# Late pieces of a spectral filter: scales by a product with ones, a fourth late piece, and earlier output units

## The chip, the cores and the metric

One core of a Trainium2 chip runs the whole program. The metric is the device time of one execution in microseconds; before the change the median of three runs is 583.74 us (583.57 to 584.98).

## The reference

Two independent halves, laid side by side in the last dimension of the output. Half A is attention with 16 query heads of 28 numbers and one shared key and value head over 2048 positions. Half B is a two-dimensional real Fourier transform of a 2048 x 448 array, a product with learned complex weights, and the transform back.

```python
# half A: S = 2048, D = 448, H = 16, Dh = 28
q = (x @ wq).reshape(B, S, H, Dh).transpose(0, 2, 1, 3)
k, v = x @ wk, x @ wv
p = softmax(einsum("bhqd,bkd->bhqk", q, k) * Dh ** -0.5)
a = einsum("bhqk,bkd->bhqd", p, v).transpose(0, 2, 1, 3).reshape(B, S, H * Dh) @ wo
# half B
X = rfft2(B_x) * (w_r + 1j * w_i)
b = irfft2(X, s=(S, D))
return concatenate([a, b], axis=-1)
```

## The kernel before

**First stage (to about 61 us).** TensorE multiplies x with the joined weights of queries, keys and values (L351). A small planner (`Plan`) orders these tasks with those of half B's first transform. Half B's input is cut into eight pieces `q` of 256 rows in the kernel's own order. A piece is folded on VectorE (`fold_part`), goes through the transform along the features on TensorE (`fa_task`, which calls `features`, L183, two halves `p`), is taken out by ScalarE, and goes through the first half of the transform along the positions (`fm_task`, which calls `fft1_mm`, L193). The result `bs` is stored to a DRAM array `t1`. `PLACES` names the products after which the pieces 0, 1 and 2 stand; piece 3 follows behind the last product, and of piece `L` = 4 only the features are done here. All of this is in float32.

**Main loop.** 256 steps: 16 groups (4 query blocks `c` by 4 head groups `g`) of 16 key blocks. A step is two score blocks (`scores`, L1317, 16 matmuls), two exps of 128 x 1024 on ScalarE (L1320) and a product with the values (`values`, L1336). Scores may run up to `PAIRS` = 9 blocks ahead. Each group gathers in one of two PSUM banks (`acc`), which alternate. When a group is done `group_out` (L1210) takes its bank out on VectorE, using a scale `scale_v`.

**Small units of work.** While a group gathers in one bank, the other may hold a filler unit: the late pieces of half B (`work["l"]`), output products (`work["w"]`, `w_unit`, L1255) and, towards the end, the transform back (`work["z"]`). `filler` says whether the bank is free, `owed` how much filler work is due by now, at the rates `EARLY` per step until the transform back has begun. All this is decided while the program is built: the loop keeps clocks for TensorE, VectorE and ScalarE, and `after(when, duration, function)` places VectorE's work at a time of that clock. Each engine then runs its list strictly in this order and waits where the real time differs.

**Late pieces.** For pieces 5, 6 and 7, in two float16 parts each: `late_top` finds each piece's largest value (L1009), `late_fold` folds (L165 to L173), `late_split` scales and splits (L1035, L1038), `late_features` multiplies (L1052, 48 matmuls), its `out` takes the bank out in two parts (L1061, L1062), `late_points` is the second transform (L1084; for piece `L` in float32) and its `out` scales and stores (L1092, L1094). The last piece starts `spectrum`: the rest of the transform, the product with the weights and the way back, all on VectorE.

**Maxima over partitions.** `bounce` writes a few columns of 128 maxima to DRAM (`md`), reads all of them back into each partition (`mw`) and reduces there (L922). It serves three times: for `late_top` (`mt`), for `largest` (`m`: values and output weights, from which `scale_v` comes) and for the spectrum (`mx`). The tile `mw` is single. SyncE issues these transfers, the query blocks (`qd` to DRAM and back into `qa`, `build_q`) and the stores of `bs`; GpSimd's queue issues the loads of weights and of the spectrum `X`.

**Output products.** Behind the last group of a block, `group_norm` sends leftover rows through DRAM (`lows`) and releases four `w_unit`s 7.0 us later by the clock.

Of the kernel before, what the change touches and what calls it, by code (L numbers as in the profile page):

```python
# [33 lines left out]
ROW = 32768.0  # L34
# [7 lines left out]
PLACES = (3, 5, 7)  # L42
# [59 lines left out]
def kernel(ctx: ExitStack, tc: tile.TileContext, t: dict):  # L102
# [32 lines left out]
    L = 4  # L135
    late, cs1 = {}, spare[1][1][:, :452].rearrange("p (j n) -> p j n", j=4)
    late["a", 4] = spare[1][0][:, 1024:1928]
    late["w", 4] = spare[0][1][:, 1416:1928]
    for q in range(5, 8):
        (one, two), o = spare[q > 5], 452 * (q > 5)  # L140
        if q < 7:
            late["x", q], late["W", q] = one[:, :1024], two[:, o:o + 512]
        late["f", q], late["A", q] = one[:, 1024:], two[:, o + 512:o + 1416]
# [99 lines left out]
    with tc.tile_pool(name="f1", bufs=2) as f1[0], tc.tile_pool(name="w1", bufs=1) as w1, ExitStack() as ctx1:  # L243
# [231 lines left out]
        for q in range(4):  # L475
            xb_load(q)

        def late_start():
            late_load(5, "xW")
            late_load(6, "xW")  # L480
            late_load(4, "w")
# [66 lines left out]
        for c in range(1, NC):  # L548
            for g in range(NG):
# [37 lines left out]
                if n in PLACES:  # L587
# [5 lines left out]
                    if q + 3 <= L:  # L593
                        xb_load(q + 3)
# [13 lines left out]
        fa_task(3, 0)  # L608
        fa_task(3, 1)
        ts = add(DVE, 0.2, lambda: terms(1, NC), kmb_, *(reds[a, b] for a in range(1, NC) for b in range(NG)))  # L610
        fm_task(2)
# [13 lines left out]
        fa_task(4, 0)  # L625
# [10 lines left out]
        fm_task(3)  # L636
# [3 lines left out]
        def last_features():  # L640
            pas[4, 1] = spin(2, 226)
            features(pas[4, 1], ff[4], 1)
# [84 lines left out]
        nc.vector.tensor_copy(late["a", 4][:, 1], pas[4, 1])  # L727
# [187 lines left out]
    def bounce(m, then, cols=2):  # L915
        d = dp.tile([128, cols], F32, name=f"md{cols}", bufs=2)
        nc.sync.dma_start(d, m[:, :cols])
        w = view(ap.tile([128, 384], F32, name="mw", bufs=1), 128, cols)
        nc.sync.dma_start(w, d.rearrange("(o a) b -> o a b", o=1).to_broadcast([128, 128, cols]))

        def go():
            V.tensor_reduce(m[:, :cols], w.rearrange("p a b -> p b a"), axis=AX.X, op=ALU.max)  # L922
            V.tensor_scalar(m[:, :cols], m[:, :cols], 1e-30, None, op0=ALU.max)
            then(m)
        after(clk["dve"] + 14.0, 1.0 if cols < 3 else 3.0, go)
# [76 lines left out]
    tops = {}  # L1002

    def late_top(qs):

        m = ap.tile([128, 8], F32, name="mt", bufs=1)
        V.memset(m, 0.0)
        for n, q in enumerate(qs):
            V.tensor_reduce(m[:113, n:n + 1], late["x", q][:113], axis=AX.XY, op=ALU.max, apply_absolute_value=True)  # L1009

        def fix(m):
            for n, q in enumerate(qs):
                tops[q] = ap.tile([128, 2], F32, name=f"t{q}", bufs=1)
                V.tensor_scalar(tops[q][:, 1:2], m[:, n:n + 1], 1.0 / ROW, None, op0=ALU.mult)
                V.reciprocal(m[:, 4:5], m[:, n:n + 1])
                V.tensor_scalar(tops[q][:, 0:1], m[:, 4:5], 4096.0, None, op0=ALU.mult)
# [4 lines left out]
    folded = set()  # L1021

    def late_fold(q, part=0):
        fold_part(late["x", q][:113], late["f", q][:113], part)
        if part < 2:
            after(clk["dve"], (1.22, 1.4)[part], late_fold, q, part + 1)
# [5 lines left out]
    def late_split(q, n):  # L1032
        f, x, scale = late["f", q][:113], late["F", q][:113], tops[q][:113, 0:1]
        if n == 0:
            V.tensor_scalar(x[:, 0], f, scale, None, op0=ALU.mult)  # L1035
            after(clk["dve"], 1.25, late_split, q, 1)
        else:
            STT(x[:, 1], f, scale, x[:, 0], op0=ALU.mult, op1=ALU.subtract)  # L1038
            work["l"].extend([late_features(q, 0), late_features(q, 1)])

    THREE = (0, 0), (0, 1), (1, 0)

    def late_features(q, p):
        def go(b):
# [10 lines left out]
            if q < 7 and p:  # L1055
                after(clk["pe"] + 1.8, 1.22, late_fold, q + 1)

        def out(b):
            a, pa = late["A", q][:, p], view(bank[b], 2, 226)
# [7 lines left out]
    def late_ready(q, p):  # L1067
        work["l"].insert(len(points), late_points(q, p))
        points.append((q, p))

    bsl, points = {}, []

    def late_points(q, p):
        def go(b):
            if q > L:
                points.remove((q, p))
# [9 lines left out]
            after(clk["pe"] + LAG, 0.6, out, b)  # L1086
        def out(b):
# [475 lines left out]
```

## Time and profile before

| | |
|---|---|
| profiled execution | 584.45 us; its span 582.7 us |
| TensorE (PE) busy | 571.4 us, 98% |
| ScalarE (ACT) busy | 512.7 us, 88% |
| VectorE (DVE) busy | 406.2 us, 70% |
| GpSimd (POOL) busy | 110.0 us, 19% |
| mean granted TensorE clock | 0.997 |
| HBM read, written | 44.64 MB, 19.98 MB |

A matmul in float32 leaves two records, one in float16 leaves one. Matmuls are pipelined, so durations of neighbours overlap; a distance from start to start tells more than a duration. A row of the timeline gives start, duration, engine, line, operation, tiles, and in brackets the idle time before it with what ended it. Rows that begin with two times and a colon give a stretch: its length, the busy time of PE, PEld, DVE, ACT and POOL with counts, then the granted TensorE clock, the DMA share and GB/s. The names of tiles that lie in shared memory (`spoh`, `spol`) are those of the buffer, not of the piece.

### The profile page before, as it was taken

What the parts mean: (1) busy time and instruction counts of PE and PEld (TensorE: products, weight loads), DVE (VectorE), ACT (ScalarE), POOL (GpSimd) and SP (SyncE); (2) the same over time, 40 slices, a digit from 0 to 9 for tenths busy, and PEclk for the clock granted to TensorE, in tenths of its full rate; (3) what the DMA queues carried; (4) which work ended last, traced back from release to release, by engine and by line L of the source; (5) the groups of instructions that cost most, each with busy time, mean ns of one, the idle gap of its engine ahead of it and who ended that gap; (6) DMA issues with size and microseconds to landing.
All of it is one profiled execution on the core that took longest, in us unless ns stands there. A gap on an engine that the chain in (4) does not pass through costs nothing.

```text
span 582.7 us, 20949 instructions
## 1 busy us (share of the span) xinstructions
PE 571.4 (98%) x9085; PEld 303.2 (52%) x9085; DVE 406.2 (70%) x775; ACT 512.7 (88%) x579; POOL 110.0 (19%) x199
## 2 busy tenths in 40 slices
PE   9999998999999999999999999999999999999996
PEld 7877543545454443444444444445555555555654
DVE  5996586789630999999898887845365743366544
ACT  4644897899999999999999999999999887899982
POOL 1023220121312012212111211133201321011110
PEclk9999999999999999999999999999999999999999
DMA  8864774244436202143302020456323342212111
GB/s 309 274 200 139 226 189 158 93 122 113 156 76 184 85 20 66 50 146 98 89 27 64 24 77 26 152 212 199 105 98 117 108 129 71 88 59 72 41 54 65
DMA packets 38935, 66.74 MB, mean 115 GB/s; under 512 B 7188, under 2 KB 29084, under 8 KB 38832
## 3 DMA queue, kind: packets, MB, share of 16 engines
q1 hardware_dynamic: 30008, 39.38, 20.9%
q0 software_dynamic: 8688, 25.76, 15.1%
q8 instruction: 72, 1.18, 0.9%
q14 instruction: 23, 0.19, 0.1%
q10 hardware_dynamic: 144, 0.23, 0.1%
HBM read 44.64 MB, written 19.98 MB: 111 GB/s over the span
## 4 chain that ended last, share of the span: by engine, by line
PE 77%; DMA 5%; DVE 4%; issue 1%; ACT 1%; SPq 0%; POOL 0%; DVEq 0%; ACTq 0%; POOLq 0%
PE banks L1317 34%; PE banks L1336 33%; PE banks L1255 6%; DMA mw<-md 2%; PE banks L1153 2%; PE banks L1179 2%; DMA qd<-qh 1%; DVE peaks L899 1%; DMA sd<-qraw 1%; DMA wo<-wo 0%; PE banks L1052 0%; DVE spoh L1038 0%; PE banks L1084 0%; DMA md<-mt 0%; ACT yb L1267 0%
## 5 line engine op out<-in xcount | busy, mean ns | idle before, releaser
L1320 ACT ACTIVATE p<-banks 128x1024 f32<-128x1024 f32 x512 | 477.0, 1101 | 29.7 <-PE banks L1317 29.2
L1317 PE MATMUL banks<-qa,ka 128*32 128x512 f16 x4096 | 277.1, 380 | 0.6 <-PEq L651 0.4
L1336 PE MATMUL banks<-p,vs 128*32 128x512 f32 x2048 | 268.9, 594 | 0.0
L1317 PEld LDWEIGHTS <-ka 128*32 128x32 f16 x4096 | 129.6, 96 | 168.8 <-issue 125.3
L1336 PEld LDWEIGHTS banks<-p,vs 128*32 128x32 f32 x2048 | 70.1, 110 | 43.0 <-issue 2.0
L1255 PE MATMUL banks<-woh,o 128*32 128x448 f16 x464 | 39.7, 353 | 1.2 <-DMA o<-lows 1.2
L1215 POOL DMA_DIRECT2D sd<-qraw x15 | 9.8, 651 | 154.1 <-DVE qraw L1210 154.0
L1255 PEld LDWEIGHTS <-o 128*32 128x32 f16 x720 | 23.8, 97 | 26.0 <-issue 19.6
L1223 POOL DMA_DIRECT2D R<-rd x60 | 30.5, 516 | 35.7 <-DMA rd<-rs 35.6
L865 DVE SCALAR_TENSOR_TENSOR X<-w,X 128x226 f32<-128x226 f32 (+2 forms) x72 | 34.0, 473 | 2.4
L1260 DVE TENSOR_SCALAR ya<-banks,scales 128x448 f32<-128x448 f32 x12 | 8.2, 684 | 25.5 <-PE banks L1255 25.4
L1186 DVE TENSOR_SCALAR w<-banks,scales 128x256 f32<-128x256 f32 x16 | 7.7, 484 | 25.9 <-PE banks L1179 25.8
L1210 DVE TENSOR_SCALAR qraw<-banks,scales 128x512 f32<-128x512 f32 x15 | 11.2, 749 | 20.4 <-PE banks L1336 20.4
L1255 PE MATMUL banks<-wol,o 128*32 128x448 f16 x256 | 24.8, 352 | 0.0
L1221 POOL DMA_DIRECT2D rd<-rs x15 | 8.2, 549 | 84.4 <-DVE rs L1220 72.7
L351 PE MATMUL banks<-xh,wqh 128*128 128x512 f32 x64 | 24.0, 406 | 0.0
L355 ACT ACTIVATE qraw<-banks 128x512 f32<-128x512 f32 x16 | 9.3, 596 | 16.0 <-PE banks L351 15.9
L351 PE MATMUL banks<-xh,wql 128*128 128x512 f32 x64 | 23.0, 389 | 0.0
L823 DVE TENSOR_TENSOR X<-X 128x904 f32<-128x904 f32 (+2 forms) x10 | 9.1, 906 | 18.2 <-DMA X<-t 18.2
L858 DVE SCALAR_TENSOR_TENSOR w<-X 128x113 f32<-128x113 f32 (+2 forms) x56 | 17.6, 354 | 0.1
L351 PE MATMUL banks<-xl,wqh 128*128 128x512 f32 x48 | 17.3, 390 | 0.0
L939 DVE TENSOR_TENSOR w<-X,wf 128x904 f32<-128x904 f32 x16 | 17.0, 1097 | 0.2
(182 smaller groups left out, 556.5 us busy)
## 6 DMA issues: line engine op xcount, KB each, us to landing
qa<-qd SPq DMA_DIRECT2D x62, 128.0 KB
ob<-yo SPq DMA_DIRECT2D x16, 256.0 KB
t<-bs SPq DMA_DIRECT2D x16, 226.0 KB
w<-w POOLq DMA_DIRECT2D x8, 452.0 KB, 6.0
X<-t POOLq DMA_DIRECT2D x8, 452.0 KB, 8.0
wf<-w POOLq DMA_DIRECT2D x8, 452.0 KB, 3.9
x<-t POOLq DMA_DIRECT2D x8, 452.0 KB, 4.5
R<-rd POOLq DMA_DIRECT2D x60, 56.0 KB, 2.2
```

Of the source, the lines that this page charges most:

```text
L351: mm(pq[c, g], w[:, j, gs], x[:, j], start=(j == 0 and n == 0), stop=(j == 3 and n == 1))
L858: STT(out, y, sy, x, op0=ALU.mult, op1=ALU.add if c > 0 else ALU.subtract)
L865: todo(226 * n, lambda d=d, q=q: STT(both(d), t[0].rearrange("p r n f -> p r (n f)"), q, both(a), op0=ALU.mult, op1=ALU.add))
L939: TT(u[r], both(s), wt[k][:, r:r + 1].to_broadcast([128, 2, 452]), op=ALU.mult)
L1153: mm(pz[r, j], fb["c2", q % 2][:, x, e, j, r], fb["fi", q % 2][:, j, f], start=(n == 0), stop=(n == 2))
L1179: mm(py[m:m + 32, k].rearrange("p (j n) -> p j n", j=4), cs3[:w, kind, f, m:m + 32], fb["z", q % 2, e][:w, x, :, 64 * r:64 * r + 64], star ...
L1210: V.tensor_scalar(o, bank[b], scale_v, None, op0=ALU.mult)
L1223: nc.gpsimd.dma_start(R[32 * i:32 * i + DH], rd[i:i + 1].to_broadcast([DH, CW]))
L1255: mm(p[r:r + 32], x[c][:, g, s][:, r:r + 32], w[:, m], start=(g == 0 and n == 0), stop=(g == NG - 1 and n == 2))
L1317: mm(bank[b + h][r], ka[:, k:k + 32], qa[c, g][:, 2 * p + h], start=True, stop=True)
L1320: nc.scalar.activation(pt[i], banks[:, b:b + 2], AF.Exp, scale=SCALE / UP / UP)
L1336: mm(bank[b][32 * i:32 * i + 32], vs[:, kc], pt[2 * st + i // 2][:, i % 2], start=(kc == 0), stop=(kc == 15))
```

## The change

- `L` becomes 3 and `PLACES` 4 and 7: pieces 0 and 1 stand behind products 4 and 7, piece 2 behind the last one, and piece 3 takes the place that piece 4 had. Pieces 5, 6, 4, 7 (`SEQ`) are late; they share two sets of buffers in turn, and the inputs of 4 and 7 are loaded at the start of the main loop.
- `late_top` works on two pieces at a time. The maxima `m` of 113 partitions are multiplied with a tile of ones (four matmuls of two columns, a new unit of the main loop, put at the head of `work["l"]`), which gives each partition their sum, and the scales come from the sum instead of the maximum. `bounce` is left with its two other users.
- Each late piece's fold is queued behind the split of the piece before it instead of behind its features.
- The first load of the filter weights is queued later (20.0 instead of 14.0), output units are released 8.0 instead of 7.0 behind the last normalization, and a unit may begin two steps into a group even when nothing is owed.

```diff
-PLACES = (3, 5, 7)
+PLACES = 4, 7
-    L = 4
+    L = 3
+    SEQ = 5, 6, 4, 7
...
     def late_top(qs):
-        m = ap.tile([128, 8], F32, name="mt", bufs=1)
-        V.memset(m, 0.0)
-        for n, q in enumerate(qs):
-            V.tensor_reduce(m[:113, n:n + 1], late["x", q][:113], axis=AX.XY, op=ALU.max, apply_absolute_value=True)
-        def fix(m):
-            for n, q in enumerate(qs):
-                tops[q] = ap.tile([128, 2], F32, name=f"t{q}", bufs=1)
-                V.tensor_scalar(tops[q][:, 1:2], m[:, n:n + 1], 1.0 / ROW, None, op0=ALU.mult)
...
-        bounce(m, fix, 3)
+        m = ap.tile([128, 4], F32, name="mt")
+        n = len(qs)
+        for i, q in enumerate(qs):
+            V.tensor_reduce(m[:113, i:i + 1], late["x", q][:113], axis=AX.XY, op=ALU.max, apply_absolute_value=True)
+        def go(b):
+            for r in range(0, 128, 32):
+                mm(bank[b][r:r + 32, :n], ones[:113, r:r + 32], m[:113, :n], start=True, stop=True)
+            after(clk["pe"] + LAG, 0.6, out, b)
+        def out(b):
+            t = ap.tile([128, 2, 2], F32, name="tops")
+            V.tensor_scalar(t[:, 0, :n], bank[b][:, :n], 1e-30, 2.0 ** -12, op0=ALU.max, op1=ALU.mult)
+            free[b] = clk["dve"] + 0.1
+            V.tensor_scalar(t[:, 1, :n], t[:, 0, :n], 4096.0 / ROW, None, op0=ALU.mult)
+            V.reciprocal(t[:, 0, :n], t[:, 0, :n])
...
+        after(clk["dve"] + 0.2, 0.0, work["l"].appendleft, (0.1, go))
...
-                after(clk["dve"] + 7.0, 0.0, work["w"].extend, [w_unit(c, k) for k in range(4)])
+                after(clk["dve"] + 8.0, 0.0, work["w"].extend, [w_unit(c, k) for k in range(4)])
...
-    after(14.0, 0.0, weight_top, 0)
+    after(20.0, 0.0, weight_top, 0)
-    for n, size in (("x", 1024), ("W", 512)):
-        shaped(n, 7, ap.tile([128, size], F32, name=n + "7", bufs=1))
-        late_load(7, n)
-    after(6.0, 3.4, late_top, (5, 6, 7))
-    after(6.1, 1.22, late_fold, 5)
+    ones = ap.tile([128, 128], F32, name="one", bufs=1)
+    after(2.0, 0.2, V.memset, ones, 1.0)
+    for q in SEQ[2:]:
+        for n, size in (("x", 1024), ("W", 512)):
+            shaped(n, q, ap.tile([128, size], F32, name=f"{n}{q}", bufs=1))
+            late_load(q, n)
+    after(6.0, 2.4, late_top, SEQ[:2])
+    after(6.1, 1.22, late_fold, SEQ[0])
+    after(28.0, 2.4, late_top, SEQ[2:])
...
+        if st % 16 == 2 and work["w"] and not fb:
+            owed = max(owed, 0.01)
```

By the order of the built programs the filler units of the first groups stand so (number of value steps ahead of the unit). Before: the two point units of piece 4 at 0 and 4, then features at 18 and 19, and further late units up to 51; the first output unit at 84. After: a point unit of piece 3 at 0, the first product with ones at 4, a point unit at 6, features at 8, points at 11, features at 13, the second product with ones at 19, and further late units up to 54; the first output unit at 85.

SyncE at the start of the main loop, before, from the load of the feature matrix on (`x_976`, `W_978` are the inputs of piece 7):

```order
L212 DMA spol<-cs 128x904
L212 DMA x_976<-xb 128x1024
L212 DMA W_978<-fz 128x1024
L226 DMA qd<-qh 128x512
L226 DMA qd<-ql 128x512
L229 DMA qa_79<-qd 32x4x512 x4
L917 DMA md_1092<-mt 128x3
L919 DMA mw<-md_1092 128x384
L917 DMA md_1158<-m 128x2
L919 DMA mw<-md_1158 128x256
L206 DMA t_83<-bs 256x1x226 x2
```

The same place after (`x_911`, `W_913` belong to piece 4, `x_915`, `W_917` to piece 7):

```order
L213 DMA spol<-cs 128x904
L213 DMA x_911<-xb 128x1024
L213 DMA W_913<-fz 128x1024
L213 DMA x_915<-xb 128x1024
L213 DMA W_917<-fz 128x1024
L227 DMA qd<-qh 128x512
L227 DMA qd<-ql 128x512
L230 DMA qa_79<-qd 32x4x512 x4
L916 DMA md<-m 128x2
L918 DMA mw<-md 128x256
L207 DMA t_83<-bs 256x1x226 x2
```

The trip of `mt` is gone, two loads came in ahead of `qd`, and the store of `bs` behind `mw` is now that of piece 3, from which GpSimd's first four loads of `X` read.

VectorE around the scales from `largest` and the emptying of group 0's bank, before (L922 to L800 make the scales, L1035 and L1038 are the two splits of piece 5, L1210 empties the bank):

```order
L1035 TENSOR_SCALAR spoh<-spoh,t_1357 113x1024
L922 TENSOR_REDUCE m<-mw 128x2
L923 TENSOR_SCALAR m<-m 128x2
L793 TENSOR_SCALAR m<-m 128x1
L794 TENSOR_SCALAR m<-m 128x2
L795 TENSOR_TENSOR scales<-m 128x1
L796 RECIPROCAL m<-m 128x2
L797 COPY scales<-m 128x1
L798 TENSOR_SCALAR scales<-scales 128x1
L799 TENSOR_TENSOR scales<-scales,m 128x1
L800 TENSOR_TENSOR scales<-scales 128x1
L1038 SCALAR_TENSOR_TENSOR spoh<-spoh,t_1357 113x1024
```

What stands ahead of those scales after (L1042 is the second split of piece 5, L1067 and L1068 take its first features out, L1100 its first points, L921 begins the scales):

```order
L1042 SCALAR_TENSOR_TENSOR spoh<-spoh,tops 113x1024
L1067 TENSOR_SCALAR spol<-banks 128x452
L1068 SCALAR_TENSOR_TENSOR spol<-banks,spol 128x452
L166 TENSOR_TENSOR spoh<-spoh 113x16x32 x2
L168 TENSOR_TENSOR spoh<-spoh 113x512
L169 TENSOR_TENSOR spoh<-spoh 113x512
L1100 TENSOR_SCALAR bs<-banks,tops 128x4x113
L171 TENSOR_TENSOR spoh<-spoh 113x256
L172 TENSOR_TENSOR spoh<-spoh 113x256
L173 TENSOR_TENSOR spoh<-spoh 113x256
L174 TENSOR_TENSOR spoh<-spoh 113x256
L921 TENSOR_REDUCE m<-mw 128x2
```

And what stands between those scales and the emptying of the bank after (L1008 finds the maxima of pieces 4 and 7, L898 that of a block of weights, L1039 and L1042 split piece 6, L1219 empties the bank):

```order
L1008 TENSOR_REDUCE mt<-x_911 113x1
L1008 TENSOR_REDUCE mt<-x_915 113x1
L898 TENSOR_REDUCE peaks<-w 128x1
L1039 TENSOR_SCALAR spoh<-spoh,tops 113x1024
L773 TENSOR_SCALAR woh<-wo,scales 128x448
L775 SCALAR_TENSOR_TENSOR wol<-wo,scales,woh 128x448
L1067 TENSOR_SCALAR spol<-banks 128x452
L1068 SCALAR_TENSOR_TENSOR spol<-banks,spol 128x452
L219 TENSOR_SCALAR qt<-qraw,mask,cvec 128x512
L220 CAST qh<-qt 128x512
L221 TENSOR_TENSOR ql<-qt,qh 128x512
L1042 SCALAR_TENSOR_TENSOR spoh<-spoh,tops 113x1024
```

L1219 is the next row. The whole first late piece moved ahead of the scales, and two reductions, a peak, a first split and an eviction moved in between the scales and the emptying of the bank.

More of the change, by code (lines that the diff above doesn't have):

```diff
@@ L133, in spin @@
         return view(bank[next(turn) % 6], *dims)
-    L = 4
+    L = 3
+    SEQ = 5, 6, 4, 7
     late, cs1 = {}, spare[1][1][:, :452].rearrange("p (j n) -> p j n", j=4)
[L137 to L141, printed above, removed]
+    late["a", L] = spare[1][0][:, 1024:1928]
+    late["w", L] = spare[0][1][:, 1416:1928]
+    for i, q in enumerate(SEQ):
+        (one, two), o = spare[i % 2], 452 * (i % 2)
+        if i < 2:
             late["x", q], late["W", q] = one[:, :1024], two[:, o:o + 512]
@@ L474 @@
         ident_ = load_const("ident", [128, 128])
-        for q in range(4):
+        for q in range(L + 1):
             xb_load(q)
         def late_start():
-            late_load(5, "xW")
-            late_load(6, "xW")
-            late_load(4, "w")
+            for q in SEQ[:2]:
+                late_load(q, "xW")
+            late_load(L, "w")
         late_ = add(SP, 2.4, late_start, xbl[3], kb=1800, due=45.0)
@@ L635 @@
                          cm, ident_)
[L636 removed]
+        fm_task(2)
         add(PE, 1.2, turn_values_all, users[-6], ident_, *krow_, *fetched["v"], bt_)
@@ L1025, in late_fold @@
         if part < 2:
-            after(clk["dve"], (1.22, 1.4)[part], late_fold, q, part + 1)
+            after(clk["dve"] + 0.8, (1.22, 1.4)[part], late_fold, q, part + 1)
         else:
@@ L1039, in late_split @@
             work["l"].extend([late_features(q, 0), late_features(q, 1)])
+            if q != SEQ[-1]:
+                after(clk["dve"] + 2.0, 1.22, late_fold, SEQ[SEQ.index(q) + 1])
     THREE = (0, 0), (0, 1), (1, 0)
@@ L1054, in go @@
             after(clk["pe"] + LAG, 1.3, out, b)
-            if q < 7 and p:
-                after(clk["pe"] + 1.8, 1.22, late_fold, q + 1)
         def out(b):
+            i = SEQ.index(q)
+            assert i < 2 or (SEQ[i - 2], p) in gone
             a, pa = late["A", q][:, p], view(bank[b], 2, 226)
@@ L1067, in late_ready @@
     def late_ready(q, p):
-        work["l"].insert(len(points), late_points(q, p))
-        points.append((q, p))
-    bsl, points = {}, []
+        work["l"].insert(len(ready), late_points(q, p))
+        ready.append((q, p))
+    bsl, gone = {}, set()
     def late_points(q, p):
         def go(b):
+            gone.add((q, p))
             if q > L:
-                points.remove((q, p))
+                ready.remove((q, p))
             pb = view(bank[b], 2, 226)
```

60 lines of the change are left out of this document (29 added, 31 removed).

## The prediction

> **What bounds the kernel now.** I read the busy times first, then the waits of the bottleneck engine, then the rows at the one place where it stands still. TensorE (PE) is almost never idle and ScalarE (ACT) comes next:
>
> ```profile
> PE 571.4 (98%) x9085; PEld 303.2 (52%) x9085; DVE 406.2 (70%) x775; ACT 512.7 (88%) x579; POOL 110.0 (19%) x199
> ```
>
> So the time is PE's work plus the few microseconds in which PE is slow or stands. A step of the main loop (16 score matmuls, 8 records of the value matmul) takes PE 1.72 us when nothing holds it (116.28 to 118.00 below). Where there is no other work, exp on ACT holds it: 79.70 to 96.18 is nine steps in 16.48 us, 1.83 each. The place to see is right behind that:
>
> ```profile
> 61.70 1.05 PE L1317 MATMUL banks<-qa,ka 128*32 128x512 f16 x16 [0.42 <-PEq L651]
> ...
> 64.96 1.04 PE L1336 MATMUL banks<-p,vs 128*32 128x512 f32 x8
> ...
> 71.19 0.95 PE L1084 MATMUL banks<-spoh,spol 128*32 128x226 f32 x16
> ...
> 79.70 0.61 PE L1336 MATMUL banks<-p,vs 128*32 128x512 f32 x4
> ...
> 96.18 1.04 PE L1336 MATMUL banks<-p,vs 128*32 128x512 f32 x8
> 100.12 0.80 PE L1052 MATMUL banks<-spol,spoh 113*32 113x113 f16 x48 [2.90 <-DVE qraw L1210]
> 100.73 2.22 PE L1317 MATMUL banks<-qa,ka 128*32 128x512 f16 x24
> 102.70 1.96 PE L1336 MATMUL banks<-p,vs 128*32 128x512 f32 x8
> 104.40 0.97 PE L1052 MATMUL banks<-spol,spoh 113*32 113x113 f16 x48
> 105.18 1.49 PE L1317 MATMUL banks<-qa,ka 128*32 128x512 f16 x24
> 106.47 1.05 PE L1336 MATMUL banks<-p,vs 128*32 128x512 f32 x8
> ...
> 116.28 1.05 PE L1336 MATMUL banks<-p,vs 128*32 128x512 f32 x8
> ...
> 118.00 1.04 PE L1336 MATMUL banks<-p,vs 128*32 128x512 f32 x8
> ```
>
> PE wants to put a late piece's features (L1052) into the accumulator bank of group 0 and must wait until VectorE (DVE) has emptied it (L1210). Behind the wait the clock is halved:
>
> ```profile
> 102.00:104.00 2.00, 2.00 (x20) 0.69 (x15) 1.32 (x3) 2.00 (x3) 0.00 (x0) 0.50 0.43 130
> ```
>
> (the third number from the right, the granted clock: 0.50). From 96.18 to 106.47 PE does two value steps (1.72), six score blocks of 8 matmuls (a quarter of a step each, 2.58) and two feature units (0.61 each): 5.52 us of work in 10.29, so 4.77 us are lost. Why DVE was late, from DVE, the chain of work and the SyncE queue (SPq):
>
> ```profile
> 66.81 2.35 DVE L1009 TENSOR_REDUCE mt<-spoh 113x1 f32<-113x1024 f32 x2
> 73.09 1.22 DVE L1009 TENSOR_REDUCE mt<-x 113x1 f32<-113x1024 f32 x1 [3.94 <-DMA x<-xb]
> 75.95 2.07 DVE L788 TENSOR_REDUCE m<-w 128x1 f32<-128x896 f32 x2
> 88.00 0.74 DVE L1035 TENSOR_SCALAR spoh<-spoh,t 113x1024 f16<-113x1024 f32 x1
> 93.43 0.42 DVE L922 TENSOR_REDUCE m<-mw 128x2 f32<-128x256 f32 x1 [4.69 <-DMA mw<-md]
> 95.39 1.28 DVE L1038 SCALAR_TENSOR_TENSOR spoh<-spoh,t 113x1024 f16<-113x1024 f32 x1
> 99.33 0.74 DVE L1210 TENSOR_SCALAR qraw<-banks,scales 128x512 f32<-128x512 f32 x1
> 101.07 1.09 DVE L899 TENSOR_REDUCE peaks<-w 128x1 f32<-128x904 f32 x1
> 102.72 0.63 DVE L1062 SCALAR_TENSOR_TENSOR spol<-banks,spol 128x452 f16<-128x452 f32 x1
> ```
>
> ```profile
> 65.98 8.08 DMA qd<-qh
> ...
> 76.30 2.23 DMA md<-mt
> ...
> 88.68 4.66 DMA mw<-md
> ```
>
> ```profile
> 78.93 0.42 SPq L917 DMA_DIRECT2D md<-m  x1
> ```
>
> Two trips through DRAM go through one queue and one buffer: first the late pieces' maxima (mt), then the maxima of values and output weights (m). The second write is issued at 78.93 and its read only at 88.68, 9.7 us later, and DVE, strictly in order, stands 4.69 us for it.
>
> **The change part by part.** Offsets from the first score matmul are written T0 (61.70 before).
>
> *One piece less in the first stage.* PE runs there without a gap:
>
> ```profile
> 40.25 1.76 PE L183 MATMUL banks<-spol,f 113*32 113x113 f32 x64
> 41.95 0.99 PE L193 MATMUL banks<-a,fw 64*64 64x226 f32 x16
> 42.87 0.50 PE L351 MATMUL banks<-xh,wqh 128*128 128x512 f32 x1
> ```
>
> From the start of the features (40.25) to the next L351 (42.87) one piece costs 2.62, and one such set of rows goes. All the rest of that stage hangs on PE. Term: -2.62.
>
> *The same piece in the main loop*, as two feature units and two point units (PE, starts to starts):
>
> ```profile
> 165.43 0.80 PE L1052 MATMUL banks<-spol,x 113*32 113x113 f16 x48
> 166.04 1.48 PE L1317 MATMUL banks<-qa,ka 128*32 128x512 f16 x24
> ...
> 168.19 0.77 PE L1084 MATMUL banks<-spol,W 128*32 128x226 f16 x24
> 168.77 0.59 PE L1317 MATMUL banks<-qa,ka 128*32 128x512 f16 x5
> ```
>
> 2 x 0.61 + 2 x 0.58 = +2.38. The two products with ones are new, four matmuls of two columns each. Nearest row, one product with four columns:
>
> ```profile
> 52.30 0.28 PE L521 MATMUL banks<-prod,blk 128*128 128x4 f32 x2
> ```
>
> Side by side in their four column groups 0.28, one after another 1.1; I take 0.4, near the first, since other units of four such blocks overlap. Twice: +0.8 (0.6 to 2.2).
>
> *Slack taken up.* Before, nothing but scores and values ran between 79.70 and 96.18, and ACT held PE for 9 x 0.11 = 0.98. Now five small units stand between steps 4 and 19: a product with ones (0.4), the float32 point unit that stood at step 3 (L1084 at 71.19, about 0.8 of its 0.95), two feature units and a point unit, 3.0 us in all, more than the slack. Term: -0.98. The piece's cost is thus partly hidden; where late units end (step 54) ACT binds PE as it did before from step 51, and I change nothing there.
>
> *No trip for mt.* DVE loses the 3.94 wait for the seventh piece and the third reduction, so m is ready about 5 us earlier, at T0 + 11.3 (before, L788 ended at 78.0 = T0 + 16.3). But its write does not leave earlier, because of what stands ahead of it on SyncE. In the rows of SyncE shown with the change the pair for mt is gone and 768 KB (x and W of one more piece) came in ahead of qd. The queues moved 269 GB/s while these loads ran:
>
> ```profile
> 62.00:72.00 10.00, 9.84 (x156) 4.64 (x152) 5.39 (x9) 9.59 (x11) 1.65 (x3) 1.00 0.89 269
> ```
>
> so qd lands 2.9 us later, at T0 + 12.4 + 2.9, the four qa issues take 2.2 (74.06 to 76.30), and md leaves at T0 + 17.5 (before T0 + 17.2). [...] From there md takes between 2.23 (first trip) and 9.7 (second). GpSimd's queue had four X loads of 452 KB in flight beside the second; these now include the piece that is stored behind mw in SyncE's rows, so they start later. I take 3, and mw 4.7: data at T0 + 25.2.
>
> When does DVE ask for it? By its rows shown with the change, the first late piece is split (L1042), evicted (L1067) and half through its points (L1100) ahead of L921; before, its two splits stood around the corresponding L922. L1100 needs the point unit that PE runs after 11 value steps: T0 + 3.3 (64.96) + 11 x 1.72 + 2.4 of small units = T0 + 24.6; with about 2 us of eviction and fold L921 is due near T0 + 26.7, with 1.5 to spare. From it to the end of the emptying of the bank (L1219, before L1210) the list has: the scales (93.43 to 95.39, 1.96), two reductions (2.35), one peak, one first split, one eviction (about 3.0 by L899, L1035 and twice L1062) and the work of 95.39 to 100.07 (4.68): 12.0, T0 + 38.7. PE needs the bank first for the second product with ones, after 19 steps: T0 + 3.3 + 32.7 + 3.0 = T0 + 39.0. So the 4.77 goes. Behind it DVE's list is full for some 30 steps and each unit waits for the eviction of the last, so I put +1.0 (0 to 2) for it, in which I also count this later stall (and drop it as a term, -0.72):
>
> ```profile
> 123.41 0.70 PE L1052 MATMUL banks<-spol,spoh 113*32 113x113 f16 x40 [0.72 <-DVE spoh L1038]
> 227.39 0.37 PE L1255 MATMUL banks<-woh,o 128*32 128x448 f16 x4 [1.19 <-DMA o<-lows]
> ```
>
> *Output units.* The first waited 1.19 for rows through DRAM (second row); they are now released 1 us later: -0.9 (0 to -1.2). Beginning them at step 2 of a group costs and gains nothing: the same 2.09 us in every 16 steps. The filter's spectrum comes some five steps later, so the final units crowd towards the end; PE is full there either way: 0 (-0.3 to +1).
>
> Sum: -2.62 + 2.38 + 0.8 - 0.98 - 4.77 - 0.72 + 1.0 - 0.9 = **-5.8 us**. The profiled execution took 584.45 (span 582.7, the rest lies around it and stays), 0.71 above the median of the runs, and would take 578.6; against the median of 583.74 I forecast **577.9**.
>
> **The rivals.** (a) The remaining trip still comes late and the stall stays about as it was: if md takes 7 to 8 us, PE stands some 3 us and the clock falls again. Then -5.8 - 1.0 + 4.8 = -2.0: 581.7. For it: 9.7 in the trace, and 768 KB more. Against it: the X loads are held back. The halved clock followed a wait of only 2.90. The Trainium skill, "TensorE: Matmul & The Clock Gate", section "Why this matters for your kernels", asks for no idle gap above about 3 us; the trace agrees with 2.90 and 0.50, and by either a 1 us wait stays at full clock.
> (b) Slower: md takes the full 9.7 or more, and mw lands near T0 + 33, over 6 us behind its place. DVE carries everything behind L921, so PE stands 7 us and runs 2 to 3 us more at half clock: -6.8 + 9.5 = +2.7, 586.4. It turns slower where wait and cold clock exceed 6.8, about 4 us behind its place. For it: DVE's in-order list; against: no DMA of that size took so long without the X loads.
> (c) The first stage does not shorten, because a load or the branch ends it: +2.6, 580.5. Against: PE has no wait there but 0.42 at the branch.
>
> **How the numbers follow.** Forecast 0.64, (a) 0.20, (c) 0.06, (b) 0.07, a gain eaten by small waits to within 0.3% (1.75 us, about what a measurement can tell from no change) 0.03. (a) and (c) are mostly faster than 582.0: faster 0.85, same 0.08, slower 0.07. The forecast's own terms give 575.7 to 579.7; to hold 8 in 10 the range goes up into (a): 575.4 to 581.6.
>
> **What would show it.** Right: first score near 59.0; no PE wait above 1.5 us behind a bank's emptying; clock 1.00 between 90 and 110; L921 without a wait; the first output unit without one. Wrong: a wait of L921 above 2 us with 0.50 behind it (a or b), or a first score later than 60.

## The result and the profile after

The changed kernel takes 580.07 us (median of 12 runs, 578.89 to 582.33) against 583.9 us for the kernel before beside it: ratio 0.9925, 95% interval 0.9903 to 0.9947, about 4.4 us faster. The forecast was 577.9 with a range of 575.4 to 581.6; the sign and the range hold, and the median lies 2.2 us above the forecast. The profiled execution took 579.96 us, its span is 578.2. The medians below leave out three executions in a slower state: one each of e3_both and e12_pad82 (745 us, granted clock near 0.75) and one of e5_before_banks (589.63 us). Line numbers moved: scores L1326, values L1345, late features L1058, late points L1091, the emptying of a group's bank L1219, output units L1264.

PE's busy row and its timeline where the forecast wanted the first score near 59.0:

```profile
PE 568.2 (98%) x9165; PEld 297.0 (51%) x9165; DVE 412.0 (71%) x779; ACT 510.1 (88%) x575; POOL 108.9 (19%) x199
```

```profile
57.46 0.99 PE L184 MATMUL banks<-spol,f 113*32 113x113 f32 x32
60.61 2.68 PE L1326 MATMUL banks<-qa,ka 128*32 128x512 f16 x24 [2.17 <-DVE spoh L726]
63.06 1.48 PE L1091 MATMUL banks<-spoh,spol 128*32 128x226 f32 x16
...
65.23 1.03 PE L1345 MATMUL banks<-p,vs 128*32 128x512 f32 x8
```

The last features end at 58.45 instead of 61.27, 2.82 us earlier. But PE then stands 2.17 us until VectorE's copy L726, and it runs at half clock behind that (0.50 in the window from 62 to 64 below, third number from the right). The first value step is at 65.23, before at 64.96: the first stage gave nothing. The copies that PE waits for, on VectorE, and the first of them before the change:

```profile
57.96 0.69 DVE L722 COPY vs<-banks 128x512 f32<-128x512 f32 x1 [2.15 <-DVEq L650]
58.68 1.22 DVE L507 TENSOR_TENSOR ka<-kf,ka 32x1024 f16<-32x1024 f32 x1
59.93 0.63 DVE L726 COPY spoh<-banks 128x452 f32<-128x452 f32 x1
```

```profile
60.25 0.69 DVE L723 COPY vs<-banks 128x512 f32<-128x512 f32 x1 [1.75 <-PE banks L617]
```

The name behind the 2.15 (`DVEq`, VectorE's sequencer) points at the branch, which both kernels pass here. Most of that wait is older than the change, though: the same copy waited 1.75 before, for the turned values that PE makes ahead of the last features.

At the old stall, and at the next one, PE and the windows:

```profile
94.12 1.04 PE L1345 MATMUL banks<-p,vs 128*32 128x512 f32 x8
94.98 1.05 PE L1326 MATMUL banks<-qa,ka 128*32 128x512 f16 x16
96.30 1.06 PE L1345 MATMUL banks<-p,vs 128*32 128x512 f32 x8 [0.28 <-DVE spol L1068]
98.05 1.04 PE L1345 MATMUL banks<-p,vs 128*32 128x512 f32 x8
...
100.63 0.22 PE L1012 MATMUL banks<-mt,one 113*32 113x2 f32 x8
100.69 1.04 PE L1326 MATMUL banks<-qa,ka 128*32 128x512 f16 x16
...
109.02 1.04 PE L1345 MATMUL banks<-p,vs 128*32 128x512 f32 x8
112.53 0.80 PE L1058 MATMUL banks<-spol,spoh 113*32 113x113 f16 x48 [2.47 <-DVE bs L1100]
113.14 1.49 PE L1326 MATMUL banks<-qa,ka 128*32 128x512 f16 x24
114.44 1.05 PE L1345 MATMUL banks<-p,vs 128*32 128x512 f32 x8
```

```profile
62.00:64.00 2.00, 2.00 (x26) 0.94 (x20) 0.00 (x0) 2.00 (x3) 0.43 (x1) 0.50 0.89 213
94.00:98.00 4.00, 3.73 (x56) 1.46 (x52) 3.86 (x8) 4.00 (x6) 0.00 (x0) 1.00 0.03 11
112.00:114.00 2.00, 1.47 (x64) 1.10 (x67) 2.00 (x6) 0.13 (x1) 0.00 (x0) 1.00 0.13 29
```

The stall of 4.77 us is gone, the clock is 1.00 there, and a product with ones delays the next scores by 0.06 us (100.63 to 100.69). Instead PE loses 2.65 us between 109.02 and 114.44 (5.42 for 2.77 of work). Why, from VectorE, GpSimd and SyncE:

```profile
87.98 0.44 DVE L921 TENSOR_REDUCE m<-mw 128x2 f32<-128x256 f32 x1
99.00 0.75 DVE L1219 TENSOR_SCALAR qraw<-banks,scales 128x512 f32<-128x512 f32 x1
107.56 0.45 DVE L773 TENSOR_SCALAR woh<-wo,scales 128x448 f16<-128x448 f32 x1 [4.06 <-DMA wo<-wo]
111.80 0.68 DVE L1100 TENSOR_SCALAR bs<-banks,tops 128x452 f32<-128x452 f32 x1
```

```profile
87.38 2.12 POOL L807 DMA_DIRECT2D X<-t  x4 [12.98 <-DMA t<-bs]
100.04 0.60 POOL L1224 DMA_DIRECT2D sd<-qraw  x1 [10.54 <-DVE qraw L1219]
104.15 0.56 POOL L1225 DMA_DIRECT2D rs<-sd  x1 [3.51 <-DMA sd<-qraw]
104.70 1.06 POOL L770 DMA_DIRECT2D wo<-wo  x2
```

```profile
74.20 0.38 SPq L916 DMA_DIRECT2D md<-m  x1
81.68 0.34 SPq L918 DMA_DIRECT2D mw<-md  x1
```

VectorE waits 4.06 us for a load of output weights that GpSimd issues only at 104.70, behind a store (`sd`) that waited for VectorE and a load (`rs`) that waited for that store. From there VectorE has no gap up to L1100, the eviction for which PE waits. The remaining trip's write took 7.5 us (74.20 to 81.68, until its read was issued), and yet L921 has no wait.

### The profile page after: what moved, and what is told of

It is laid out like the page before. It is cut to its first block, busy times and chain, and to the rows that moved or that the text cites. A ratio compares the mean times of both kernels' runs of the same rounds, so it can differ in the third digit from the quotient of the medians.

```text
span 578.2 us, 21096 instructions
## 1 busy us (share of the span) xinstructions
PE 568.2 (98%) x9165; PEld 297.0 (51%) x9165; DVE 412.0 (71%) x779; ACT 510.1 (88%) x575; POOL 108.9 (19%) x199
## 4 chain that ended last, share of the span: by engine, by line
PE 83%; DVE 3%; DMA 1%; ACT 1%; issue 1%; POOL 0%; ACTq 0%; DVEq 0%; POOLq 0%
PE banks L1326 37%; PE banks L1345 36%; PE banks L1264 6%; PE banks L1162 2%; PE banks L1188 2%; PE banks L1091 1%; PE banks L1058 1%; DMA sd<-qraw 1%; DVE peaks L898 1%; ACT p L1329 1%; DMA wo<-wo 0%; DVE mt L1008 0%; ACT yb L1276 0%; DVE ka L507 0%; DVE spoh L1042 0%
## 5 line engine op out<-in xcount | busy, mean ns | idle before, releaser
L1326 PE MATMUL banks<-qa,ka 128*32 128x512 f16 x4096 | 275.0, 380 | 2.2 <-DVE spoh L726 2.2
L1345 PE MATMUL banks<-p,vs 128*32 128x512 f32 x2048 | 267.4, 592 | 0.3 <-DVE spol L1068 0.3
L1326 PEld LDWEIGHTS <-ka 128*32 128x32 f16 x4096 | 126.5, 97 | 168.6 <-issue 119.9
L1345 PEld LDWEIGHTS banks<-p,vs 128*32 128x32 f32 x2048 | 68.0, 110 | 44.4 <-issue 1.2
L1264 PE MATMUL banks<-woh,o 128*32 128x448 f16 x464 | 39.8, 352 | 0.0
L1264 PEld LDWEIGHTS <-o 128*32 128x32 f16 x720 | 22.2, 97 | 27.1 <-issue 19.3
L1219 DVE TENSOR_SCALAR qraw<-banks,scales 128x512 f32<-128x512 f32 x15 | 11.2, 749 | 22.1 <-PE banks L1345 22.1
L1264 PE MATMUL banks<-wol,o 128*32 128x448 f16 x256 | 24.2, 352 | 0.0
L857 DVE SCALAR_TENSOR_TENSOR w<-X 128x113 f32<-128x113 f32 (+2 forms) x56 | 17.5, 355 | 0.1
```

Source lines behind the costliest of these rows:

```text
L857: STT(out, y, sy, x, op0=ALU.mult, op1=ALU.add if c > 0 else ALU.subtract)
L1219: V.tensor_scalar(o, bank[b], scale_v, None, op0=ALU.mult)
L1264: mm(p[r:r + 32], x[c][:, g, s][:, r:r + 32], w[:, m], start=(g == 0 and n == 0), stop=(g == NG - 1 and n == 2))
L1326: mm(bank[b + h][r], ka[:, k:k + 32], qa[c, g][:, 2 * p + h], start=True, stop=True)
L1345: mm(bank[b][32 * i:32 * i + 32], vs[:, kc], pt[2 * st + i // 2][:, i % 2], start=(kc == 0), stop=(kc == 15))
```

## The experiments

All times are device medians beside the kernel before in the same set of runs (583.2 to 584.31). Where two kernels are compared at one place, the starts of the value steps in their traces are used.

**1. The bank of the first score.** The counter that deals the six small banks counts two less for a piece less, so the last features came to lie in bank 0, which the first score writes.

```diff
-    turn = count()
+    turn = count(2)     # e1_banks (changed kernel); count(4) in e5_before_banks (kernel before)
```

> The changed kernel with one number different: the counter that deals the six small banks in the first stage starts two further on, so that, as before the change, the last features lie in bank 2 and the small values in bank 1, which the second and third score block need, instead of bank 0 and 5, of which bank 0 is the first score block's. Theory: in the changed kernel the first score (60.61 in its profile) waited 2.17 us for VectorE's copy of the last features out of that bank (59.93 + 0.63), not for the branch or a load. Then the first score stands near 58.9 to 59.2 with a wait under 0.7 us, the clock between 60 and 64 is above 0.9 instead of 0.50, and the first value step is near 62.3 instead of 65.23. Of these 2.9 us a part is given back about the second product with ones, because the two trips of the maxima (7 us each way before their data) don't move up by as much: I expect 1 to 3 us less than the changed kernel, 577 to 579. Rival: the copies of VectorE or the branch end the stage whatever the bank: first score still at 60 to 61, time within 0.5 us of the changed kernel.

Measured 578.83, ratio 0.9909 (0.9874 to 0.9944): in the interval of the changed kernel. PE:

```profile
58.66 0.61 PE L1326 MATMUL banks<-qa,ka 128*32 128x512 f16 x6 [0.43 <-DMA t<-bs]
60.83 2.32 PE L1326 MATMUL banks<-qa,ka 128*32 128x512 f16 x18 [1.56 <-issue]
```

The first score is at 58.66 as the theory had it, but after six matmuls PE stands 1.56 us, marked "issue": for nothing that the profile shows. The clock halves all the same (0.53 from 60 to 62), and the first value step is at 64.66, not near 62.3. So the bank was a wait, with a second one hidden behind it.

> The kernel before, with one number different: the counter of the small banks starts four further on, which puts the last features into bank 0, the first score block's, as in the changed kernel. Theory: the first score waits for VectorE's copy of the last features (62.22 + 0.63 in the profile of before) and starts near 62.9 instead of 61.70; the idle time of about 1.6 us before it may or may not halve the clock. The kernel becomes 1.0 to 3.0 us slower, 585 to 587. Rival: the bank is not what holds the first score: first score at 61.7, the time within 0.6 us of before.

Measured 582.8, ratio 0.9987 (0.9954 to 1.002): no difference, where 585 to 587 was expected. Yet the collision is there. PE, then VectorE:

```profile
62.45 2.38 PE L1317 MATMUL banks<-qa,ka 128*32 128x512 f16 x24 [1.63 <-DVE spoh L727]
...
67.07 1.03 PE L1336 MATMUL banks<-p,vs 128*32 128x512 f32 x8
```

```profile
91.07 0.42 DVE L922 TENSOR_REDUCE m<-mw 128x2 f32<-128x256 f32 x1 [1.51 <-DMA mw<-md]
```

From the end of the features (60.82) the first value step takes 6.25 us, against 3.69 before: 2.56 are lost. In this execution they come back at the stall of the two trips: VectorE waits 1.51 for `mw` instead of 4.69, and PE has no wait between 96 and 106. So in the kernel before, a loss of 2.6 us in the first stage cost nothing that the medians show, because a trip with its own time stood behind it. That reason rests on one trace, and its execution (580.74) is the fastest of the eleven, which reach up to 587.37.

**2. The branch behind the first stage.** e9_order takes e2_wo (below) and moves the copy L726 ahead of L507; e10_nobranch takes both edits of e3_both and leaves out the branch (the test of the scores' bound, and the rare path).

> The kernel e2_wo (changed kernel with the earlier load of output weights, 577.34 us) with VectorE's copy of the last features moved ahead of its 1.22 us subtraction for the keys: the bank of the first score is emptied 1.2 us earlier. Theory that the bank alone holds the first score: it starts at 58.9 instead of 60.11, and the first value step is 1.2 to 2.5 us earlier than 65.85; total 575 to 576.3. Rival, after e1_banks: TensorE has only some twelve instructions to run behind the branch that it passes there (in e1_banks six matmuls ran from 58.66 and it then stood 1.56 us until 60.83 for nothing that the profile shows); then six or so matmuls run near 58.9, the next at 60.2 to 60.8 as before, and the total is within 0.8 us of e2_wo.

> The kernel e3_both (banks as before, earlier load of output weights, 576.78 us) without the branch behind the first stage: the test of the scores' bound and the rare path that rescales queries and keys are left out, all else is computed. Theory: the 1.56 us for which TensorE stood behind its first six score matmuls in e1_banks, and the 2.15 us for which VectorE stood at the branch, are the branch (the engines run on only when the code behind it has come); then the scores run from about 58.4 without a gap above 0.7 us, the clock stays at 1.00 between 58 and 64, the first value step is at 61.5 to 62.5 instead of 64.66, and the total is 573 to 575.5. Rival: the stop is something else (a transfer or a bank): it stays without the branch, the first value step is later than 63.5, and the total is within 0.7 us of e3_both.

e9_order: 576.67, ratio 0.9852 (0.9820 to 0.9884), not to be told from e2_wo. e10_nobranch: 574.13, ratio 0.9817 (0.9786 to 0.9848), 2.5 below e3_both's median; the two intervals overlap at their ends (0.9836 to 0.9848). PE in the first, then in the second:

```profile
59.87 0.61 PE L1326 MATMUL banks<-qa,ka 128*32 128x512 f16 x6 [0.91 <-DVE spoh L723]
61.85 2.32 PE L1326 MATMUL banks<-qa,ka 128*32 128x512 f16 x18 [1.37 <-issue]
...
65.95 1.24 PE L1345 MATMUL banks<-p,vs 128*32 128x512 f32 x8
```

```profile
58.14 1.05 PE L1252 MATMUL banks<-qa,ka 128*32 128x512 f16 x16
60.09 0.62 PE L1252 MATMUL banks<-qa,ka 128*32 128x512 f16 x8 [0.91 <-DVE spoh L652]
...
62.15 1.05 PE L1271 MATMUL banks<-p,vs 128*32 128x512 f32 x8
```

Again six matmuls and a stop; without the branch and the code in it there is no stop, only a wait of 0.91 for a bank, and the first value step is at 62.15. So the stop comes with the branch. It is not the branch as such, though: the kernel before has the branch and no stop. Does the place of the code behind it count? e11_pad18 has the edits of e1_banks, e2_wo and e9_order and 18 idle matmuls in the warm-up, e12_pad82 has 82.

```diff
+        for _ in range(18):
+            mm(nothing[:32, :32], idle[:, :32], idle[:, :32], start=True, stop=True)
```

> The branch stays. Changed kernel with the banks as before, the earlier load of output weights, the copy of the last features ahead of the keys' subtraction, and 18 idle matmuls of 32 by 32 columns in the warm-up at the start (36 instructions, under 1 us, output never read). Between before and after the code behind the branch moved by 164 instructions on TensorE (80 matmuls and 80 weight loads of the piece, 4 others), which is 36 more than a block of 128. Theory: where the code behind the branch falls in the blocks in which it is fetched decides; with 36 instructions added it falls as it did before the change (if blocks of 128 count), and the stop of 1.4 to 1.6 us behind the first six score matmuls is gone: score matmuls run without a gap above 0.5 us from about 59, the first value step is 4.0 us or less behind the end of the last features (3.7 before, 6.5 in e1_banks), and the kernel takes 573.5 to 575.5. Rival: the stop comes with any branch that is passed at this point of the stage, whatever the place of the code: 1.2 us or more of idle time within the first three score blocks, 575.5 to 577.5.

> As e11_pad18 with 82 idle matmuls (164 instructions) instead of 18, so that the code behind the branch falls in the same place of blocks of 256 and of 128 as in the kernel before; they cost some 2 to 5 us of the warm-up, of which about 1 us is waited anyway, so the stage starts 1 to 4 us later and the total is read with that. Theory: no stop behind the first score matmuls, first value step 4.0 us or less behind the end of the last features; total 574.5 to 579, by the warm-up's length. If this kernel has no stop and e11_pad18 has one, blocks of 256 count; if both have one, the place of the code is not it. Rival: stop of 1.2 us or more here too.

e11_pad18: 575.76, ratio 0.9873 (0.9835 to 0.9910); e12_pad82: 576.59, ratio 0.9884 (0.9851 to 0.9918). PE:

```profile
59.69 1.48 PE L1328 MATMUL banks<-qa,ka 128*32 128x512 f16 x24 [0.43 <-DMA t<-bs]
...
62.82 1.04 PE L1347 MATMUL banks<-p,vs 128*32 128x512 f32 x8
```

```profile
60.55 1.48 PE L1328 MATMUL banks<-qa,ka 128*32 128x512 f16 x24 [0.43 <-DVE vs L724]
...
63.68 1.04 PE L1347 MATMUL banks<-p,vs 128*32 128x512 f32 x8
```

No stop in either, the clock stays at 1.00, and the first value step is 3.56 us behind the end of the features (59.26 and 60.12): a little better than the 3.69 before the change. So with the code shifted by 36 or by 164 instructions the stop is gone. Two things keep this short of a proof: both shifts were chosen to restore the old place and no other was run, and the edits of e1_banks and e9_order were not run together without a shift, though each of the two kernels had the stop. That the stop is a fetch of instructions fits, but is not shown. By the traces' record of DMAs a block of 16 KB on the queue named "instruction" landed at 59.56 in e1_banks and at 60.39 in e9_order, and PE went on 1.27 and 1.46 us later. But e12_pad82 has such a block from 60.37 to 61.82 and no stop.

In the medians the 3.1 us at this place (65.95 to 62.82) do not show between e9_order and e11_pad18, whose intervals overlap. The profiled execution of e9_order is the slowest of its five (578.69). The two of the five with a mean granted clock of 1.00 took 575.25 and 575.70, as fast as the four of e11_pad18 with 1.00 (574.39 to 576.70). So by these clocks the halving comes in some executions of one kernel and not in others, and a trace shows only one of them.

**3. The load of output weights.**

```diff
-        after(at, 0.0, wo_load, g)
+        after(at - (g == 2), 0.0, wo_load, g)     # e2_wo; e3_both has the banks of e1_banks too
```

> The changed kernel, with the load of the third group of output weights issued one microsecond earlier by the planner's clock, so that in GpSimd's queue it stands ahead of a store (sd) that waits for VectorE and the load behind it (rs). Theory: the wait of 2.47 us of TensorE at 109 to 114 of the changed kernel comes from that queue: the weights were issued at 104.70, VectorE stood 4.06 us for them and the eviction behind it came late. Then both waits go (under 0.5 us) and the time falls by 2.0 to 2.6 us, to about 577.5 to 578. Rival: VectorE's list of work is simply too long there: its wait for the weights goes, but TensorE still stands 1 us or more between 105 and 116, and the time falls by less than 1.2 us.

> Both edits together (banks of the first stage as before the change, and the third load of output weights ahead of the store on GpSimd). Theory: two separate losses, so the gains add but for what the trip of the second maxima gives back: 3.5 to 5 us less than the changed kernel, 575 to 576.5. If the trip of the maxima (its write took 7.5 us in the changed kernel) is the next to be late, VectorE waits 1 to 3 us for it near 88 and TensorE stands near 95 with a halved clock; then only 2 to 3 us less, 577 to 578. Rival (neither edit touches a bound): within 0.7 us of the changed kernel.

e2_wo: 577.34, ratio 0.9874 (0.9839 to 0.9909), 2.7 below the changed kernel's median, where 2.0 to 2.6 was expected; all six executions (575.91 to 578.15) are faster than the twelve of the changed kernel. GpSimd, VectorE and PE:

```profile
96.20 0.54 POOL L770 DMA_DIRECT2D wo<-wo  x1 [7.06 <-DVE wol L775]
```

```profile
104.28 0.44 DVE L773 TENSOR_SCALAR woh<-wo,scales 128x448 f16<-128x448 f32 x1
```

```profile
110.74 0.80 PE L1058 MATMUL banks<-spol,spoh 113*32 113x113 f16 x48
```

Both waits are gone: the load now leaves at 96.20. The rival (VectorE's list is too long there) has fallen: with the load early nothing is lost between 106 and 113. e3_both: 576.6, ratio 0.9871 (0.9836 to 0.9905), no better than e2_wo alone. The stop behind the branch would explain that, but there is no trace of e3_both that could show it.

**4. The fourth late piece.** Four kernels keep pieces 0 to 3 in the first stage and 5, 6, 7 late as before, and the rest of the change. They differ in when the filter behind the pieces starts and in the spacing of the weights' reductions, so no pair of kernels here differs by the piece alone.

```diff
-    L = 3
-    SEQ = 5, 6, 4, 7
+    L = 4
+    SEQ = 5, 6, 7
...
-        t0 = clk["dve"] + 3.0
+        t0 = clk["dve"] + 18.6     # e4c_no_piece, e4d_no_piece
```

> The changed kernel without one of its three parts: the fourth late piece. Five pieces go through the first stage as before the change and three run late, while the scales come from a product with ones and output units start two steps into a group; the reductions of the output weights follow each other 2 us closer so that they end in time. Theory: the gain of the change comes from the trip through DRAM that is gone (4.8 us of stall and slow clock), the output units (0.9 to 1.5) and the later stall, and the fourth late piece brings nothing, since what it takes out of the first stage (2.8 us) is lost to the bank at the first score and what it adds in the main loop is partly hidden: this kernel then takes 577 to 580, as fast as the changed kernel or up to 3 us faster. Rival: the moved piece carries 2 us or more of the gain: this kernel takes 582 to 584.

> The kernel e4_no_piece (the changed kernel with five pieces in the first stage and three late, as before the change) again, with one planned time different: the first two loads of the filter's last stage are taken to land 22 us after their issue instead of 9, so the units behind them are released later. In e4_no_piece the filter came to that stage one group earlier than in the changed kernel, GpSimd's queue held a store behind a wait of 15.9 us, and TensorE stood 5.27 us for the first of these units at 382 to 388, with a halved clock behind it; up to step 160 of 256 that kernel was 3.4 us ahead of the changed one. Theory: without this accident the kernel takes 576.5 to 578.5, 1.5 to 3.5 us less than the changed kernel, so that the fourth late piece is no part of the gain but costs. Rival: the 3.4 us at step 160 are only units that are done later and come back by the end: 579.5 to 582, no better than the changed kernel.

> The kernel e4_no_piece (three late pieces instead of four, the rest of the change kept) once more, now with the filter behind the late pieces started as late as in the changed kernel (15.6 us later by the planner's clock, the reductions of the weights spaced as in the changed kernel): in e4_no_piece and e4b_no_piece TensorE stood 5.27 and 4.49 us between 380 and 397 because GpSimd's queue held the filter's store and loads behind a store that waited 16 us for VectorE, and both kernels, 2.5 to 3.4 us ahead of the changed kernel at step 160 with the same work done, lost 8 us there. Theory (the late piece costs and the rest of the change carries the gain): the stall near 390 is gone and the kernel takes 576 to 578.5, 1.5 to 4 us less than the changed kernel. Rival (the early lead is only order and is given back in the filter's last stages): 579.5 to 582.

> Three late pieces and five in the first stage, as before the change, with the rest of the change kept: as e4c_no_piece (the filter behind the late pieces starts as late as in the changed kernel), but with the reductions of the weights spaced as in e4_no_piece, so that GpSimd issues its X loads behind the trip of the maxima again. In e4c_no_piece they were issued at 73.66, ahead of the trip's write (74.94), which then took 12.0 us, and VectorE stood 3.58 us for it; in e4_no_piece, with the loads at 84.92, it took 7.1 us. Theory 1 (the late piece itself brings nothing): no wait of VectorE for the trip and none of TensorE above 2 us before 120 or between 370 and 420; at step 160 as e4b_no_piece, 2 to 3 us ahead of the changed kernel, and 576.5 to 578.5 in all. Theory 2 (its lead at step 160 is given back by crowded units later): as far ahead at step 160, yet 579.5 to 581. If TensorE stands 2 us or more at another place again, the total says nothing on the piece and the place is told.

| kernel | us | ratio, 95% interval | step 160 | what stood in the way |
|---|---|---|---|---|
| changed | 580.07 | 0.9925 (0.9903 to 0.9947) | 366.47 | |
| e4_no_piece | 584.83 | 1.0004 (0.9984 to 1.0025) | 363.09 | PE 5.27 at 388 |
| e4b_no_piece | 583.99 | 0.9994 (0.9975 to 1.0013) | 364.00 | PE 4.49 at 396 |
| e4c_no_piece | 581.67 | 0.9963 (0.9942 to 0.9984) | 366.50 | PE 2.91 at 98.8 |
| e4d_no_piece | 578.22 | 0.9898 (0.9873 to 0.9922) | 364.72 | |

The first three missed the times that their theories gave, each by another stall; e4c_no_piece came at its rival's time, but not for the rival's reason. In e4_no_piece the filter comes a group earlier, and its store (`t<-X`) and load (`x<-t`) queue on GpSimd behind a store that waits 15.9 us for VectorE:

```profile
363.52 0.73 POOL L1225 DMA_DIRECT2D sd<-qraw  x1 [15.90 <-DVE qraw L1220]
...
367.33 0.78 POOL L980 DMA_DIRECT2D t<-X  x1
...
378.67 0.74 POOL L1135 DMA_DIRECT2D x<-t  x1 [10.02 <-DMA t<-X]
```

e4b_no_piece told the planner that these loads land later; PE's wait only moved. In e4c_no_piece the X loads left ahead of the trip's write, which then took 12.0 us instead of 7.5 (GpSimd, SyncE, VectorE, PE):

```profile
73.66 2.12 POOL L809 DMA_DIRECT2D X<-t  x4
```

```profile
74.94 0.81 SPq L918 DMA_DIRECT2D md<-m  x1
86.97 0.34 SPq L920 DMA_DIRECT2D mw<-md  x1
```

```profile
91.54 0.54 DVE L923 TENSOR_REDUCE m<-mw 128x2 f32<-128x256 f32 x1 [3.58 <-DMA mw<-md]
```

```profile
98.83 1.07 PE L1346 MATMUL banks<-p,vs 128*32 128x512 f32 x8 [2.91 <-DVE spol L1070]
```

That is the late trip of rival (a), though without a fall of the clock. e4d_no_piece has neither stall, only 1.48 at 109.38, and is not slower than the changed kernel: 1.75 us ahead at step 160, 1.69 at the last step. Its total is lower by 0.27% in the ratios, but the intervals overlap. So a kernel with the rest of the change and without the fourth late piece is no slower: the piece is no visible part of the gain here. That it costs is not shown. The changed kernel still has its two repairable losses in this comparison (the bank and the load of output weights), and with the second repaired (e2_wo, 0.9874) it is not behind e4d_no_piece (0.9898), whose 1.48 is left in.

## Why the prediction was right or wrong

The sign is right, and the stall for which the change was made is gone. That the number lies in the range owes something to luck. 580.07 lies above the 579.7 that was given as the upper end of the forecast's own terms, in the part added for rival (a), which did not happen. (Nor do 575.7 to 579.7 follow from the bounds stated for the terms: added up, these give 576.1 to 582.2.) The time is nearest to rival (c), a first stage that does not shorten (580.5), and one of the signs named for "wrong" came: the first score is later than 60, at 60.61. A PE wait above 1.5 us behind a bank's emptying came too (2.47). The other signs came out as right: clock 1.00 between 90 and 110, L921 and the first output unit without a wait. Term by term:

- **A piece less in the first stage (-2.62).** The features end 2.82 earlier: the price was right. "All the rest of that stage hangs on PE" was the step that failed. The first score also hangs on VectorE's three copies (2.54 in a row) and on the dealing of banks, which put the last features into the bank that it writes; the stop behind the branch (1.4 to 1.6 in e1_banks and e9_order) lay behind that. The copies themselves came only 2.29 earlier (57.96 instead of 60.25). The first value step came 0.27 later instead of 2.6 earlier. Rival (c) named a load or the branch as what could end the stage, with 0.06; its price of +2.6 was near the 2.89 that the term was off, but what came first was the bank. Which bank the last features lie in stands in the listing of instructions and not in the profile.
- **The piece in the main loop (+2.38), the products (+0.8).** The work was as priced but for the products: 0.06 each instead of 0.4, with all eight records of one within 0.22 us.
- **Slack (-0.98).** Over steps 2 to 16 the time that is not work fell from 1.01 to 0.50 (starts of value steps less the work between them, which counts 0.76 for the float32 point unit): 0.51 instead of 0.98.
- **The stall (-4.77, -0.72).** Right: over steps 16 to 21 time that is not work went from 4.93 to 0.03, and over 24 to 30 from 1.03 to 0.01. The step under it was not: the write of `m` was taken at 3 us and took 7.5. Another error made up for it. The write was forecast to leave 17.5 us behind the first score, held back by the two new loads, and left after 13.6 (74.20), so its read was issued at 21.1 instead of 20.5. That is luck. L921 had no wait, because what stood ahead of it on VectorE ended only at 87.98, 27.4 behind the first score (26.7 in the forecast). The emptying of the bank ended at 99.75, after 39.1 (38.7 in the forecast). That the X loads are held back was right (87.38); with them ahead of the write (e4c_no_piece) it took 12.0 us and a stall came back. That the trip's removal alone ended the stall is not shown: e5_before_banks has both trips and no PE wait there either.
- **VectorE's full list (+1.0).** It cost 2.65, outside the stated 0 to 2, and by another mechanism: GpSimd's queue. The forecast followed DMAs on SyncE and the X loads on GpSimd, but not the loads of output weights behind `sd` and `rs`.
- **Output units (-0.9).** The first one starts without a wait at 225.46, as forecast; over steps 60 to 84 time that is not work fell from 2.59 to 0.89, more than forecast. How much of it is the release by 1 us was not tried apart.

Up to step 160 both kernels have done the same units, apart from the piece. There the changed one is 2.98 ahead: +0.27 at the first value step, +2.93 of work (2.50 of units, 0.43 of scores done ahead), -6.18 of time that is not work. From there to the end it gains 1.5 more (4.5 of the spans), which no term of the sum had and whose cause is open. The removal of the trip was never run alone; the stall is absent from the traces of the changed kernel and of e4d_no_piece, which has the trip removed and one piece less late.

The best of the kernels that compute everything by median is e11_pad18 (575.76), by ratio e9_order (0.9852); with e2_wo and e3_both they are one group, 7.0 to 7.7 us below the medians of the kernel before beside them, and the times do not tell them apart.

## What to carry to other kernels

A shorter stage is worth what the first instruction behind it gains: look which bank, which copy and which branch that instruction waits for, before you count its work. Where a transfer with its own time stands behind a loss, the loss may be free, and a gain ahead of it too: in the kernel before, 2.6 us lost ahead of such a transfer left the median where it was. An engine's in-order queue must be read through for every load that moves, and behind each store that waits for another engine.

## What the runs showed of the hardware

- **The same branch goes with a stop of TensorE or without one.** With the changed kernel's code PE stood 1.37 us (e9_order) and 1.56 us (e1_banks) after six matmuls; it did not with 36 or 164 instructions more ahead of the branch (e11_pad18, e12_pad82), in the kernel before, or without the branch (e10_nobranch). Why is open.
- **The length of a wait alone does not halve the clock.** Behind waits of 1.63 (e5_before_banks) and 2.17 (changed kernel) at the first scores the granted clock fell to 0.50; around 2.47 at 110 to 112.5 (changed kernel) and behind 2.91 at 98.8 (e4c_no_piece) it stayed at 1.00. By the Trainium skill, "TensorE: Matmul & The Clock Gate", section "Why this matters for your kernels", there should be no idle gap above about 3 us if the clock is not to drop. The trace agrees with the two later waits and not with the two at the first scores. What else decides is open, but it differs between executions of one kernel: the mean granted clock was 1.00 in three of the six of e1_banks and 0.996 to 0.997 in the others. In the traces' clock records the halving lasts 3.41 us in the kernel before, the changed kernel and e1_banks, and 6.83 in e2_wo; the full clock ahead of it lasts 95.57, 54.61, 54.61 and 54.61 us, whole multiples of 3.41 too. So the changes fall on a grid of 3.41 us, and the grid lies at another place in each execution: full clock first began 5.75, 6.12, 5.52 and 4.66 us into the span. Behind the wait in e4c_no_piece:

```profile
98.00:100.00 2.00, 1.17 (x16) 0.46 (x20) 1.97 (x4) 0.00 (x0) 0.00 (x0) 1.00 0.00 0
100.00:102.00 2.00, 2.00 (x36) 0.89 (x32) 1.93 (x4) 1.57 (x2) 0.00 (x0) 1.00 0.12 42
```

- **A write of 1 to 1.5 KB to DRAM took from 2.2 us (`mt` before the change) to 12.0 (e4c_no_piece)** until the read behind it could be issued. With the X loads issued within 1.3 us of it, the write of `m` took 9.4, 9.7 and 12.0 (e5_before_banks, before, e4c_no_piece); with them at least 3 us behind its end, 5.3 to 8.1 (ten kernels, e12_pad82 and e1_banks at the ends; 7.5 in the changed kernel).
